# A convolution, Fourier and MLP kernel on one core: the front work of batches 2 to 7 put on batch 1's step table

## The chip, the cores and the metric

The kernel runs on one core of a Trainium2 chip. The metric is device time in microseconds (us). Before the change the median of three runs was 1313.27 us (1310.71 to 1316.33). One execution was profiled; its own time is 1317.36 us and its trace spans 1315.6 us.

## The reference, cut to what matters

For each of 8 batches of 4224 tokens with 192 channels, a causal convolution of 7 taps (softmax weights, one set per head of 24 channels) is followed by a two-dimensional Fourier transform whose real part is added back, a normalisation and a two-layer MLP with a residual:

```
x   = lightweight_conv(x, softmax(weight))          # (8, 4224, 192)
mix = real(fft(fft(x, axis=1), axis=2))
u   = x + mix
un  = (u - mean(u)) / sqrt(var(u) + 1e-6)            # over the 192 channels
out = u + relu(un @ w_ch1) @ w_ch2                   # 192 -> 768 -> 192
```

## The kernel before, in words

Work is cut into batches `b` (0 to 7) and, in each batch, nine items `it` (0 to 8). One item is 512 output tokens (item 8 has 128). A *step* `n = 9 b + it` is one pass of the loop at L882: the MLP of item `it` is its main work, and everything else is placed between the MLP's pieces. The MLP's first half (`mlp_hidden`, L665) makes six blocks `ph` of five matmuls each (L680); ScalarE writes each as `hh` (L684) and VectorE its remainder `hlo` (L685). Two PSUM buffers hold `ph`, so the sixth block cannot be computed before the fourth `hh` and `hlo` are written. The second half (`mlp_out`, L689) makes `po` (L699, L702, L705) one step later, from all six `hh` and `hlo`, adds it to `u` (L711) and stores `u` (L719). Normalisation (`un` L628, `hl` L638 and L641) and the DMA transpose of `hl` into `kt` (L651, on SyncE's queue, SP) run about two steps ahead of the MLP that reads `kt`.

The *front work* of a later batch rides in the steps of the batches ahead of it. `front(bt, rel)` (L763) says which pieces are issued in a step, by `rel = n - 9 b`:

- convolution of six window chunks (`load_windows` L323, matmuls `pc` L387, copies `xa` L395, stores to a DRAM scratch `sc` L355, squares `sq` L343) at rel -17 to -12; batch 7 does one head on VectorE instead (`conv_segments`, L403, stored by L421);
- `load_x` (L441): the scratch is read back in four pieces `xs` with another token order, four DMAs each on SP's queue (L456). The pieces share two buffers, so piece 2 can be loaded only when both splits of piece 0 are done, and piece 3 only after piece 1;
- `split_x` (L460): each piece is split in two halves into a high part `XH` (ScalarE, L472) and a low part `XL` (VectorE, L473), eight splits in all;
- `stage_a` (L479): 16 units of 12 matmuls `pa` (L490), written out as `yh` (ScalarE, L498) and `yl` (VectorE, L499). Each unit reads all of `XH` and `XL` in its columns, so none can start before the last split;
- `stage_b` (L504): matmuls `pb` (L516) into `V` (L524, L525), from rel -4 on by `b_at`.

Four tables set the steps of load, split and stage A. Batch 1 has its own (`load_1`, `split_1`, `a_1`); batches 2 to 7 use `load_at`, `split_at`, `a_at` (L752 to L754). Batch 0's are done before the loop. So batch 1's front work lies in the steps of batch 0, and that of batch 2 in the steps of batch 1. Below, "step 1 of batch 2" is item 1 of batch 2, where the front work of batch 3 has rel -8.

A scheduler turns this code into one instruction list per engine. It may move an instruction that is ready ahead of its place in the code, but each engine, and SP's queue of DMAs with it, then runs its list in order. `issue_after` keeps ScalarE's splits behind the last `hh` (L471) and, for batch 1 alone, loads behind the last transpose (L455).

## Time and profile before

| what | value |
|---|---|
| median of three runs | 1313.27 us |
| profiled execution, its own time | 1317.36 us |
| span of its trace | 1315.6 us |
| TensorE (PE) matmul busy | 1194.7 us, 91% |
| ScalarE (ACT) busy | 821.3 us, 62% |
| VectorE (DVE) busy | 746.8 us, 57% |
| GpSimd (POOL) busy | 645.0 us, 49% |
| mean granted TensorE clock | 0.961 |

The profiled execution is 1.8 us longer than its span and 4.1 us above the median. Matmuls are pipelined, so a busy PE is not a PE at its peak. Steps can be found in the trace by the first `hh` activation of each; from 429.7 us on, nine of them make batch 2. The granted clock is the share of full speed that TensorE had in a stretch.

### The profile page before, as it was taken

Reading aid. Unit: us, or ns where it says so; the run is one execution under the profiler, and the core shown is the slowest. Engines: PE = TensorE matmul, PEld = TensorE weight load, DVE = VectorE, ACT = ScalarE, POOL = GpSimd, SP = SyncE. Lnnn points to the kernel's source line nnn. Section 1 sums busy time; section 2 is a strip of 40 time slices with the busy share of each in tenths; the row PEclk is TensorE's granted clock in tenths of the full one; section 3 lists DMA queues with packets and bytes.
Section 4 is the critical chain, followed back from the end, with each engine's and each line's share of the span. In section 5 each row is a group of like instructions: output and inputs, shape, how many; then the busy total and the mean of one; then the engine's idle time right before and its main releaser. Section 6 shows DMA issues by size and latency. Waiting matters only on the chain.

```text
span 1315.6 us, 30115 instructions
## 1 busy us (share of the span) xinstructions
PE 1194.7 (91%) x12224; PEld 942.4 (72%) x12224; DVE 746.8 (57%) x1635; ACT 821.3 (62%) x1562; POOL 645.0 (49%) x1052
## 2 busy tenths in 40 slices
PE   4187899997999989997999979999889998999999
PEld 4175678775878668785777858787567876778667
DVE  6765564465545655456644565456754576555444
ACT  4655786566755687557765677566755667555642
POOL 0165644564445734455445563456434675456520
PEclk9587999998999989999999989999899999999999
DMA  8945865556756556466664557545564544223321
GB/s 271 247 118 136 226 161 120 133 117 142 146 127 132 150 117 133 121 139 149 124 147 109 134 152 146 133 117 145 136 123 117 124 101 85 72 68 76 76 64 40
DMA packets 225819, 170.19 MB, mean 129 GB/s; under 512 B 119560, under 2 KB 207440, under 8 KB 225680
## 3 DMA queue, kind: packets, MB, share of 16 engines
q1 hardware_dynamic: 163408, 108.53, 35.7%
q10 hardware_dynamic: 49600, 33.77, 10.5%
q0 software_dynamic: 12672, 25.97, 7.6%
q8 instruction: 95, 1.56, 0.5%
q14 instruction: 44, 0.36, 0.1%
HBM read 83.73 MB, written 58.55 MB: 108 GB/s over the span
## 4 chain that ended last, share of the span: by engine, by line
PE 38%; POOL 18%; issue 14%; ACT 11%; DMA 8%; DVE 5%; SPq 2%; ACTq 0%; POOLq 0%; DVEq 0%
PE ph L680 14%; POOL xr L544 8%; DMA xs<-sc 6%; PE po L699 4%; PE po L705 4%; PE po L702 4%; PE pa L490 4%; POOL u L592 4%; ACT XH L472 3%; PE pq L574 3%; POOL hl L641 3%; ACT un L628 2%; PE pc L387 2%; DVE XL L473 2%; PE pb L516 2%
## 5 line engine op out<-in xcount | busy, mean ns | idle before, releaser
L680 PE MATMUL ph<-kt,W 128*128 128x512 f16 (+1 forms) x2160 | 502.4, 366 | 19.5 <-DVE hlo L685 13.2
L685 DVE SCALAR_TENSOR_TENSOR hlo<-ph,hh 128x512 f16<-128x512 f32 (+1 forms) x400 | 271.5, 679 | 347.5 <-ACT hh L684 346.3
L699 PE MATMUL po<-W,hh 128*128 128x192 f16 x1584 | 388.7, 249 | 43.8 <-ACT hh L684 36.8
L702 PE MATMUL po<-W,hh 128*128 128x192 f16 x1584 | 388.5, 248 | 0.0
L705 PE MATMUL po<-W,hlo 128*128 128x192 f16 x1584 | 384.4, 248 | 0.8 <-DVE hlo L685 0.8
L684 ACT ACTIVATE hh<-ph 128x512 f16<-128x512 f32 (+1 forms) x400 | 235.3, 589 | 187.8 <-PE ph L680 180.0
L544 POOL DMA_INDIRECT xr<-sc,rows_sb x264 | 268.3, 1016 | 136.5 <-issue 59.4
L680 PEld LDWEIGHTS <-W 128*128 128x128 f16 x2160 | 195.3, 99 | 168.1 <-issue 29.4
L641 POOL TENSOR_TENSOR hl<-un,hl 128x512 f16<-128x512 f32 (+1 forms) x144 | 127.9, 910 | 219.2 <-ACT hl L638 219.1
L699 PEld LDWEIGHTS <-hh 128*128 128x128 f16 x1584 | 156.8, 99 | 58.6 <-ACT hh L684 40.0
L592 POOL TENSOR_TENSOR u<-u,xr 128x768 f32<-128x768 f32 (+1 forms) x72 | 124.6, 1731 | 138.2 <-ACT u L591 138.1
L705 PEld LDWEIGHTS <-hlo 128*128 128x128 f16 x1584 | 156.0, 99 | 26.0 <-issue 2.4
L702 PEld LDWEIGHTS <-hh 128*128 128x128 f16 x1584 | 156.4, 99 | 22.2 <-issue 7.8
L628 ACT ACTIVATE un<-u,nm,y 128x192 f32<-128x192 f32 x256 | 120.0, 537 | 73.1 <-POOL nm L618 72.7
L387 PE MATMUL pc<-xt,band 128*120 128x144 f32 x756 | 118.9, 297 | 21.8 <-DMA band<-line_d 14.7
L472 ACT ACTIVATE XH<-xs,s_x 128x768 f16<-128x768 f32 x64 | 104.3, 1670 | 40.3 <-DMA xs<-sc 40.3
L387 PEld LDWEIGHTS pc<-xt,band 128*120 128x120 f32 x756 | 105.6, 190 | 29.5 <-issue 14.7
L473 DVE SCALAR_TENSOR_TENSOR XL<-xs,s_x,XH 128x768 f16<-128x768 f32 x64 | 102.2, 1609 | 42.4 <-ACT XH L472 37.0
L490 PE MATMUL pa<-c_sb,XH 128*128 128x128 f16 x1024 | 103.1, 223 | 18.0 <-ACT XH L472 17.4
L711 DVE SCALAR_TENSOR_TENSOR u<-po,fo,u 128x384 f32<-128x384 f32 (+1 forms) x136 | 81.8, 601 | 58.1 <-PE po L705 57.0
L499 DVE SCALAR_TENSOR_TENSOR yl<-pa,yh 99x512 f16<-99x512 f32 x128 | 85.3, 681 | 33.2 <-ACT yh L498 33.2
L490 PEld LDWEIGHTS <-XH 128*128 128x128 f16 x1024 | 82.3, 99 | 28.1 <-ACT XH L472 18.0
(125 smaller groups left out, 1454.8 us busy)
## 6 DMA issues: line engine op xcount, KB each, us to landing
out_dram<-u SPq DMA_DIRECT2D x64, 384.0 KB
xt<-in_xw_dram SPq DMA_DIRECT2D x42, 576.0 KB
sc<-xa ACTq DMA_DIRECT2D x42, 540.0 KB
xs<-sc SPq DMA_DIRECT2D x96, 192.0 KB
xs<-sc SPq DMA_DIRECT2D x32, 216.0 KB
xr<-sc,rows_sb POOLq DMA_INDIRECT x264
sc<-xa ACTq DMA_DIRECT2D x7, 450.0 KB
xt<-in_xv_dram SPq DMA_DIRECT2D x6, 504.0 KB
```

The costliest lines, as they stand in the source:

```text
L387: nc.tensor.matmul(pc[:WR, h - h0], band[:, h, :WR], xt[:, :, h * GRP : (h + 1) * GRP], start=True, stop=True,)
L490: nc.tensor.matmul(pa[:, i], x[:, at], F[:, l], start=(n == 0), stop=(n == 2))
L544: nc.gpsimd.indirect_dma_start(bt.xr[it][:, g], None, bt.sc[:S], bass.IndirectOffsetOnAxis(ap=rows_sb[:, col : col + 1], axis=0),)
L592: nc.gpsimd.tensor_tensor(u[:, :ng], u[:, :ng], xr[:, :ng], op=ALU.add)
L628: nc.scalar.activation(un[:, g], u[:, g], AF.Identity, bias=nm[:, g : g + 1], scale=y[:, g : g + 1],)
L641: nc.gpsimd.tensor_tensor(bl[:, :, o : o + n], un[:, :ng, f], hi[:, :, f], op=ALU.subtract)
L680: nc.tensor.matmul(ph[:, n], W1[:, w, ht * 128 : (ht + 1) * 128], kt[:, k], start=(i == 0), stop=(i == len(order) - 1),)
L684: anchor[0] = nc.scalar.activation(hh, ph, AF.Relu).ins
L685: nc.vector.scalar_tensor_tensor(hlo, ph, 0.0, hh, op0=ALU.max, op1=ALU.subtract)
L699: nc.tensor.matmul(po[:, g % 2], hh[:, ht, tk], W2[:, ht, 0], start=(ht == 0), stop=False)
L702: nc.tensor.matmul(po[:, g % 2], hh[:, ht, tk], W2[:, ht, 1], start=False, stop=False)
L705: nc.tensor.matmul(po[:, g % 2], hlo[:, ht, tk], W2[:, ht, 0], start=False, stop=(ht == 5),)
```

## The change

Batches 2 to 7 get the tables that only batch 1 had, and batch 1's own copies of the three tables go. Load, split and stage A of those batches stand at rel -9 to -5 where they stood at -10 to -5: the first load and the first split one step later, stage A in two steps (6 and 10 units) where it had three (4, 6 and 6).

```diff
-    load_at = {-10: [0], -9: [1, 2], -8: [3]}
-    split_at = {-9: [0, 1], -8: [2, 3, 4, 5], -7: [6, 7]}
-    a_at = {-7: range(0, 4), -6: range(4, 10), -5: range(10, 16)}
+    load_at = {-9: [0, 1], -8: [2, 3]}
+    split_at = {-8: [0, 1], -7: [2, 3, 4, 5], -6: [6, 7]}
+    a_at = {-6: range(0, 6), -5: range(6, 16)}
...
-        conv, load, split, a = (
-            (conv_1, load_1, split_1, a_1) if bt.b == 1
-            else (conv_at, load_at, split_at, a_at)
-        )
+        conv = conv_1 if bt.b == 1 else conv_at
```

In the order of instructions, nothing changes on TensorE until the steps of batch 1. Three places show what moves. In the names, `hh_2_1` and `ph_2_1_3` are item 1 of batch 2 (and its block 3), and `xs_3_2` is piece 2 of batch 3's transform input.

ScalarE in step 1 of batch 2, before, from the second `hh` to the fourth:

```order
L684 ACTIVATE hh_2_1_5994<-ph_2_1_1_6071 128x512
L472 ACTIVATE XH_106<-xs_3_1_5925,s_x3_5555 128x64x12 x2
L610 ACTIVATE sd_2_4_6229<-mv_2_4_6140,eps_68 128x4
L684 ACTIVATE hh_2_1_5994<-ph_2_1_2_6129 128x512
L472 ACTIVATE XH_106<-xs_3_2_5941,s_x3_5555 128x64x12 x2
L628 ACTIVATE un_2_3_6004<-u_2_3_5894,nm_2_3_5981,y_2_3_5978 128x192 x4
L684 ACTIVATE hh_2_1_5994<-ph_2_1_3_6167 128x512
```

The same stretch after the change:

```order
L684 ACTIVATE hh_2_1_5985<-ph_2_1_1_6062 128x512
L472 ACTIVATE XH_106<-xs_3_0_5931,s_x3_5555 128x64x12
L610 ACTIVATE sd_2_4_6221<-mv_2_4_6132,eps_68 128x4
L684 ACTIVATE hh_2_1_5985<-ph_2_1_2_6123 128x512
L472 ACTIVATE XH_106<-xs_3_0_5931,s_x3_5555 128x64x15
L343 ACTIVATE sq_4_0_6161,nrm_4_6160<-xt_4_0_5772 128x1152
L395 ACTIVATE xa_4_0_6163<-pc_4_0_0_6164 120x3x6x24
L628 ACTIVATE un_2_3_5995<-u_2_3_5857,nm_2_3_5972,y_2_3_5969 128x192 x4
L684 ACTIVATE hh_2_1_5985<-ph_2_1_3_6169 128x512
```

Before, the splits of pieces 1 and 2 stand here, and the fourth `hh` stands behind those of piece 2. After, the two splits of piece 0 stand here, and piece 2 is not split before step 2.

SP's queue over steps 1 and 2 of batch 2, before (`kt` is a transpose, `xt` a window chunk of the convolution, `out` a store of `u`):

```order
L651 DMA_TRANSPOSE kt_2_2_5930<-hl_2_2_5847 128x12x128
L330 DMA xt_4_1_5992<-in_xw_dram 128x1152
L456 DMA xs_3_2_5941<-sc_3_3843 32x8x192 x4
L456 DMA xs_3_3_6066<-sc_3_3843 32x8x192 x4
L719 DMA out_1_dram<-u_2_0_5131 128x768
L651 DMA_TRANSPOSE kt_2_3_6124<-hl_2_3_6060 128x12x128
L330 DMA xt_4_2_6251<-in_xw_dram 128x1152
L651 DMA_TRANSPOSE kt_2_4_6365<-hl_2_4_6289 128x12x128
```

And after:

```order
L651 DMA_TRANSPOSE kt_2_2_5920<-hl_2_2_5810 128x12x128
L330 DMA xt_4_1_5983<-in_xw_dram 128x1152
L456 DMA xs_3_2_6057<-sc_3_3827 32x8x192 x4
L719 DMA out_1_dram<-u_2_0_5131 128x768
L651 DMA_TRANSPOSE kt_2_3_6118<-hl_2_3_6051 128x12x128
L330 DMA xt_4_2_6243<-in_xw_dram 128x1152
L651 DMA_TRANSPOSE kt_2_4_6342<-hl_2_4_6281 128x12x128
L456 DMA xs_3_3_6094<-sc_3_3827 32x8x192 x4
```

Piece 2's loads keep their place on SP, and piece 3's move back past a store, two transposes and a window load. Pieces 0 and 1 are read at the same places of SP's list in both programs.

ScalarE in step 2, where pieces 1 and 2 are split under the new table. In the program before, batch 1 has that table, so this is step 2 of batch 0:

```order
L684 ACTIVATE hh_0_2_1581<-ph_0_2_0_1583 128x512
L472 ACTIVATE XH_106<-xs_1_1_1310,s_x1_1273 128x64x12
L395 ACTIVATE xa_2_1_1719<-pc_2_1_0_1720 120x3x6x24
L395 ACTIVATE xa_2_1_1719<-pc_2_1_3_1737 120x3x6x24
L684 ACTIVATE hh_0_2_1581<-ph_0_2_1_1623 128x512
L472 ACTIVATE XH_106<-xs_1_1_1310,s_x1_1273 128x64x12
L472 ACTIVATE XH_106<-xs_1_2_1393,s_x1_1273 128x64x12
L610 ACTIVATE sd_0_5_1777<-mv_0_5_1692,eps_68 128x4
L684 ACTIVATE hh_0_2_1581<-ph_0_2_2_1681 128x512
```

Step 2 of batch 2 after the change:

```order
L684 ACTIVATE hh_2_2_6245<-ph_2_2_0_6247 128x512
L472 ACTIVATE XH_106<-xs_3_1_5959,s_x3_5555 128x64x12
L395 ACTIVATE xa_4_1_6383<-pc_4_1_0_6384 120x3x6x24
L395 ACTIVATE xa_4_1_6383<-pc_4_1_3_6401 120x3x6x24
L395 ACTIVATE xa_4_1_6383<-pc_4_1_6_6435 120x2x6x24
L355 DMA sc_4_6159<-xa_4_1_6383 120x6x192
L684 ACTIVATE hh_2_2_6245<-ph_2_2_1_6287 128x512
L472 ACTIVATE XH_106<-xs_3_1_5959,s_x3_5555 128x64x12
L472 ACTIVATE XH_106<-xs_3_2_6057,s_x3_5555 128x64x12
L355 DMA sc_4_6159<-xa_4_1_6383 120x3x192
L610 ACTIVATE sd_2_5_6441<-mv_2_5_6356,eps_68 128x4
L684 ACTIVATE hh_2_2_6245<-ph_2_2_2_6345 128x512
```

The splits stand at the same places between the `hh`; what differs is where the convolution's third `xa` and its two stores stand. On TensorE the two programs have the same work in these steps: 80 `po` (83 in batch 0) and no `pa` in step 2, 47 `po` and 82 `pa` in step 3, 83 `po` and 110 `pa` in step 4, 72 `po` and 31 `pb` in step 5. In the old order of batch 2 the `pa` of steps 2, 3 and 4 are 61, 79 and 52.

More of the change, by code (lines that the diff above doesn't have):

```diff
@@ L751 @@
     conv_at = {r: [r + 17] for r in range(-17, -11)}
-    load_at = {-10: [0], -9: [1, 2], -8: [3]}
-    split_at = {-9: [0, 1], -8: [2, 3, 4, 5], -7: [6, 7]}
-    a_at = {-7: range(0, 4), -6: range(4, 10), -5: range(10, 16)}
+    load_at = {-9: [0, 1], -8: [2, 3]}
+    split_at = {-8: [0, 1], -7: [2, 3, 4, 5], -6: [6, 7]}
+    a_at = {-6: range(0, 6), -5: range(6, 16)}
     b_at = {-4: [0], -3: [1, 2], -2: [3], -1: [4], 0: [5, 6], 1: [7]}
     conv_1 = {-9: [4, 5]}
-    load_1 = {-9: [0, 1], -8: [2, 3]}
-    split_1 = {-8: [0, 1], -7: [2, 3, 4, 5], -6: [6, 7]}
-    a_1 = {-6: range(0, 6), -5: range(6, 16)}
     def front(bt, rel):
         units = []
-        conv, load, split, a = (
-            (conv_1, load_1, split_1, a_1) if bt.b == 1
-            else (conv_at, load_at, split_at, a_at)
-        )
+        conv = conv_1 if bt.b == 1 else conv_at
         for ch in conv.get(rel, ()):
@@ L780, in front @@
             units.append(call(scales, bt))
-        units += [call(load_x, bt, ch) for ch in load.get(rel, ())]
-        units += [call(split_x, bt, i) for i in split.get(rel, ())]
-        units += [call(stage_a, bt, t) for t in a.get(rel, ())]
+        units += [call(load_x, bt, ch) for ch in load_at.get(rel, ())]
+        units += [call(split_x, bt, i) for i in split_at.get(rel, ())]
+        units += [call(stage_a, bt, t) for t in a_at.get(rel, ())]
         return units
```

## Prediction

> **What bounds the kernel now.** I read the page first, then cut batch 2 into its nine steps (at the first `hh` of each), then asked the waits and the chain of waits of the one step that stands out. The page gives TensorE (PE) as the busiest engine, and in the costliest groups one line on the part that the change moves, the splits:
>
> ```profile
> PE 1194.7 (91%) x12224; PEld 942.4 (72%) x12224; DVE 746.8 (57%) x1635; ACT 821.3 (62%) x1562; POOL 645.0 (49%) x1052
> L472 ACT ACTIVATE XH<-xs,s_x 128x768 f16<-128x768 f32 x64 | 104.3, 1670 | 40.3 <-DMA xs<-sc 40.3
> ```
>
> ScalarE (ACT) is only 62% busy, yet stood 40.3 us before splits because a load of `xs` had not landed. The steps of batch 2 (length, busy time by engine, granted clock) show where:
>
> ```profile
> 429.70:447.50 17.80, 17.63 (x201) 13.83 (x199) 11.06 (x24) 14.84 (x28) 11.50 (x20) 1.00 0.43 116
> 447.50:473.70 26.20, 17.71 (x130) 12.30 (x129) 13.76 (x23) 16.21 (x27) 14.29 (x23) 0.80 0.68 158
> 473.70:491.30 17.60, 17.60 (x183) 14.07 (x182) 11.32 (x23) 14.60 (x26) 7.14 (x12) 1.00 0.49 120
> 491.30:509.70 18.40, 18.40 (x196) 14.86 (x194) 11.29 (x25) 13.00 (x27) 8.96 (x14) 1.00 0.73 145
> 509.70:528.90 19.20, 19.20 (x206) 15.52 (x204) 10.41 (x23) 13.22 (x27) 8.97 (x14) 1.00 0.64 143
> 528.90:545.40 16.50, 16.50 (x177) 12.82 (x175) 6.59 (x13) 7.89 (x17) 6.87 (x15) 1.00 0.57 123
> ```
>
> The first number behind the length is PE's busy time. PE fills every step but step 1, which has few matmuls (130 records) and the longest time, with the clock at 0.80. The waits in that step, and the chain of waits through it:
>
> ```profile
> PE po L699 <- ACT hh L684: 7.4, 1, 7.4
> ACT XH L472 <- DMA xs<-sc: 7.0, 1, 7.0
> ```
>
> ```profile
> 446.82 1.92 DVE XL L473
> 448.76 0.33 SPq L456
> ...
> 452.20 8.44 DMA xs<-sc
> 460.80 3.09 ACT XH L472 x2
> ...
> 466.18 0.34 PE po L699
> ...
> 470.89 0.16 PE po L699
> ```
>
> This is a loop through two buffers. `XL` of piece 0 ends at 448.7, only then may SP issue piece 2 into its buffer, piece 2's split starts at 460.80, 12 us later, and the fourth `hh` stands behind that split on ACT; `po` waits for it until 466.18. Then PE runs at half speed: one `po` takes 0.16 us until past 470.89, against 0.08 in the same chain at full clock:
>
> ```profile
> 426.08 0.08 PE po L699
> 428.56 1.08 PE ph L680 x5
> 484.66 1.49 PE pc L387 x12
> ```
>
> So step 1 is not bound by PE's work but by one load that starts too late. The rows of step 1 for batches 1, 3, 4, 5 and 6:
>
> ```profile
> 291.00:317.00 26.00, 17.55 (x130) 12.29 (x129) 13.75 (x23) 16.20 (x27) 14.29 (x23) 0.80 0.69 159
> 604.20:628.30 24.10, 16.64 (x130) 11.69 (x129) 14.40 (x26) 16.23 (x27) 14.94 (x24) 0.86 0.68 164
> 758.90:782.30 23.40, 16.29 (x130) 11.62 (x129) 14.20 (x25) 16.29 (x27) 14.63 (x24) 0.85 0.65 165
> 912.70:934.70 22.00, 16.22 (x122) 10.88 (x120) 13.51 (x22) 14.22 (x24) 13.10 (x23) 0.84 0.74 180
> 1073.10:1093.30 20.20, 15.43 (x139) 11.23 (x137) 13.20 (x23) 14.89 (x24) 15.37 (x23) 1.00 0.66 129
> ```
>
> **The witness.** The old program already runs batch 1 on the new tables, inside the steps of batch 0. Its steps 1 to 5:
>
> ```profile
> 132.10:157.40 25.30, 21.06 (x199) 16.35 (x198) 13.14 (x36) 17.59 (x34) 14.24 (x27) 0.93 0.80 215
> 157.40:173.80 16.40, 14.75 (x117) 10.46 (x116) 12.59 (x21) 14.43 (x22) 10.58 (x13) 1.00 1.10 263
> 173.80:193.80 20.00, 19.91 (x221) 16.15 (x219) 13.16 (x25) 15.85 (x29) 7.76 (x13) 1.00 0.39 107
> 193.80:215.00 21.20, 21.20 (x239) 17.29 (x237) 12.84 (x27) 15.14 (x32) 10.75 (x16) 1.00 0.55 135
> 215.00:232.30 17.30, 17.30 (x190) 13.55 (x190) 7.12 (x13) 8.43 (x18) 6.85 (x15) 1.00 0.56 124
> ```
>
> Its step 1 is no model, since there the convolution and scale of batch 1 itself are still being finished. Steps 2 to 5 have the matmuls of the new order almost to the number. Its splits on ACT (start, length, in brackets the idle time before), and the issue of piece 3 on SP:
>
> ```profile
> 145.57 3.58 ACT L472 ACTIVATE XH<-xs,s_x 128x768 f16<-128x768 f32 x2 [3.29 <-DMA xs<-sc]
> 161.01 3.16 ACT L472 ACTIVATE XH<-xs,s_x 128x768 f16<-128x768 f32 x2
> 174.33 3.15 ACT L472 ACTIVATE XH<-xs,s_x 128x768 f16<-128x768 f32 x2
> ```
>
> ```profile
> 164.27 1.78 SPq L456 DMA_DIRECT2D xs<-sc  x4
> ```
>
> The 3.29 us is piece 0, whose scratch had only just been written. The first half of piece 2 (second in the row of 161.01) and piece 3 (174.33) started without a wait.
>
> **The change part by part,** for one batch.
>
> *Step 1: the wait goes.* Piece 0 is now split here and piece 2 one step later. Whether its load is then in time, ACT's own durations tell:
>
> ```profile
> 446.69 0.94 ACT L395 ACTIVATE xa<-pc 120x432 f32<-120x432 f32 x2
> ...
> 463.80 1.85 ACT L628 ACTIVATE un<-u,nm,y 128x192 f32<-128x192 f32 x4
> 465.55 0.57 ACT L684 ACTIVATE hh<-ph 128x512 f16<-128x512 f32 x1
> 466.03 1.15 ACT L343 ACTIVATE sq<-xt 128x1152 bf16<-128x1152 f32 x1
> ...
> 467.17 0.83 ACT L638 ACTIVATE hl<-un 128x768 f16<-128x768 f32 x1
> ...
> 470.39 1.21 ACT L591 ACTIVATE u<-pq,g 128x384 f32<-128x384 f32 x3 [1.91 <-DMA out_dram<-u]
> ```
>
> From the end of piece 0's second split to piece 2's first, ACT's new list has one `sq` (1.2), two sets of `un` (3.7), two `hl` (1.7), one `u` (1.2), five `hh` (2.5, a start every 0.5), six `xa` (2.8) and both splits of piece 1 (3.1): 16.2 us without any idle time. The load needs `XL` (1.9) and the 12.0 us from 448.76 to 460.80, together 13.9. So 7.0 us go. With the stand of 7.4 us the half clock behind it goes too: from 466.18 to between 471 and the step's end at 473.7, 4.9 to 7.5 us at half speed, which is 2.4 to 3.8 us lost; I take 3.0. The Trainium skill has this as a rule ("TensorE: Matmul & The Clock Gate", Part 1): about one idle window of 3.4 us drops the clock to half. Row and rule agree on a stand of 7.4 us; by the rule a remaining stand of over 3.4 us would bring the half clock back, and the second rival below prices that from rows.
> Step 1 takes in six `pc` (1.49/12 = 0.124 us each) and four `po` (0.08) from step 0, and a little ACT work in place of two splits: 1.1 to 1.5 us, I take 1.3. So 26.2 - 7.0 - 3.0 + 1.3 = 17.5 us. Bounds: 19.2 if only the wait goes (26.2 - 7.0), and 13.8 if PE's `ph`, `po` and `pc` alone set it (30 x 0.216 + 76 x 0.083 + 8 x 0.124).
>
> *Step 0: lighter.* It hands on 12 `po` and 6 `pc`: 12 x 0.083 + 6 x 0.124 = 1.7 us, and two splits of 1.6 us each on ACT, which PE hides there. I take -1.7 (bounds 0 and -1.9, the latter with the 0.2 us in which PE is idle there).
>
> *Steps 2 to 5: fuller.* Stage A's 16 units stand in two steps, right behind the last split, so PE has less to put between. The witness: 16.4 + 20.0 + 21.2 + 17.3 = 74.9 us against 17.6 + 18.4 + 19.2 + 16.5 = 71.7. That is +3.2, and includes PE waiting in step 3 for piece 3's splits. Steps 6 to 8 keep their work: 0.
>
> *Piece 3's load on SP.* It now stands behind two transposes and waits there for `XL` of piece 1. Queued behind it are a window load, a store and the transpose for the MLP three steps on, which the next step does not need. The witness left it 10.1 us (164.27 to 174.33), and it came in time. At the 12.0 us of piece 2's load it would be 1.9 us late. I take 0, the row of the same piece at the same place, and keep 1.9 per batch for the range. POOL takes no part in load, split or stage A, and no bytes or instructions are added.
>
> *Batch 7's head on VectorE.* Its tiles share the buffers of `xs`, so it moves along, and with it the issue that holds ACT in step 3 of batch 5:
>
> ```profile
> 956.72 4.75 ACTq L421 DMA_DIRECT2D sc<-sg  x1
> ```
>
> After the change this issue stands at the end of that step, with batch 7's first read of `xs` now ahead of a transpose on SP. I take 0, since the same issue stays in ACT's list; the bounds are 4.75 us either way, once in the run.
>
> *The sum.* Step 1 now: 26.0 + 26.2 + 24.1 + 23.4 + 22.0 + 20.2 = 141.9 us over six batches. After: 17.5 in batches 1 to 4, 17.0 in 5 (narrower convolution), 16.5 in 6 (none): 103.5. That gives -38.4. Step 0: five times -1.7 = -8.5 (batch 6 has no `pc` to move). Steps 2 to 5: six times +3.2 = +19.2. Together -27.7 us, from 1317.4 to 1289.7 for the profiled execution; on the median, which lies 4.1 us lower, 1313.3 - 27.7 = 1285.6.
>
> **Rivals.**
>
> *Full relief (0.12).* PE alone sets the new steps: step 1 at 15.5, and 2 to 5 at +1. Then -(141.9 - 93.0) - 8.5 + 6 = -51.4, so 1262. For it: PE is 91% busy and fills seven steps. Against: ACT's 16.2 us in step 1 shrink by little.
>
> *ACT keeps the bound (0.20).* The splits still stand ahead of `hh` in steps 1 and 2, PE still stands three to four microseconds, and the half clock comes back as in the witness's step 1 (0.93 of 25.3, 1.8 us). Step 1 at 19.2 in all six: -26.7 - 8.5 + 19.2 = -16.0, so 1297; with 0.9 us of wait for piece 3 it is 1303.
>
> *The late load moves to piece 3 (0.08, slower).* If piece 3's four DMAs need over 14 us, ACT stands before its splits in step 3, and stage A with it. All 7.0 + 3.0 us back in five batches is +50 - 28 = +22: 1335. It decides from about 3.9 us of wait a batch (with 1.7 of clock, 5 x 5.6 = 28). Against it: the witness's unharmed 10.1 us. The Trainium skill speaks for it ("DMA: Bandwidth & Descriptors", Rules for kernel authors): issue a DMA early, wait late. By that rule a table that loads later costs time. Here the issue of pieces 2 and 3 is set by the buffer's release, 448.7 in the chain, and what the table moves is mostly the reader; the trace so far speaks against the rule's use here.
>
> *Nothing to speak of (0.06).* The scheduler keeps its own order, pieces 0 and 1 are loaded at the same places as before, and gains and the fuller steps cancel: 1313.
>
> **How the numbers follow.** My forecast, 1285.6, has 0.54. About 0.5%, 6.6 us, is what a measurement here can tell from no change. Forecast, full relief and ACT's bound are all faster by more: 0.86. The same: 0.06. Slower: 0.08. The range runs from 1266 (most of full relief) to 1304 (ACT's bound with a late piece 3); outside lie the slower rival, no change and a part of full relief.
>
> **What would show it.** In the changed profile, step 1 of batches 1 to 5 should last 16 to 19 us with the clock near 1.00, and ACT's wait for `xs` before splits should fall from 40.3 to under 15 us (the first batches keep theirs). Steps 3 and 4 should be 19 to 22 us. If step 1 shrinks and step 3 shows ACT waiting for `xs`, the third rival is right; if step 1 stays above 19 with no DMA wait, the second. I am wrong if steps 2 to 5 grow by over 8 us.

## The result and the profile after

The changed kernel takes 1300.77 us, the median of four runs (1298.91 to 1301.58), beside 1313.15 us for the kernel before on the same chip: a ratio of 0.990 with an interval of 0.988 to 0.992. Forecast were 1285.6 us, in a range of 1266 to 1304. So the direction is right and the time lies in the range, but the gain is 12.4 us where the sum gave 27.7. The profiled execution took 1301.58 us with a span of 1299.8 us, 15.8 us less than the span before. The page of the changed kernel, the busy engines and the row of the splits:

```profile
PE 1192.8 (92%) x12224; PEld 937.5 (72%) x12224; DVE 745.3 (57%) x1635; ACT 821.3 (63%) x1562; POOL 649.5 (50%) x1052
L472 ACT ACTIVATE XH<-xs,s_x 128x768 f16<-128x768 f32 x64 | 105.7, 1681 | 16.8 <-DMA xs<-sc 16.8
```

ScalarE's wait for loads ahead of splits fell from 40.3 to 16.8 us. TensorE is busy as long as before (1192.8 against 1194.7 us), so what was gained is idle time of TensorE. The steps 0 to 5 of batch 2 after the change (length, busy time by engine, granted clock), to be laid beside the six rows before:

```profile
421.50:436.10 14.60, 14.60 (x174) 11.05 (x173) 8.58 (x22) 10.82 (x24) 9.37 (x17) 1.00 0.46 130
436.10:456.80 20.70, 19.06 (x170) 15.16 (x168) 9.81 (x19) 15.29 (x28) 13.02 (x24) 1.00 0.57 128
456.80:472.90 16.10, 13.17 (x101) 8.46 (x100) 12.64 (x21) 14.26 (x23) 9.22 (x13) 1.00 1.13 194
472.90:494.60 21.70, 19.96 (x218) 15.97 (x216) 13.11 (x25) 15.73 (x28) 7.68 (x13) 1.00 0.56 139
494.60:515.90 21.30, 21.30 (x241) 17.39 (x239) 12.84 (x27) 15.19 (x32) 10.73 (x16) 1.00 0.52 137
515.90:533.10 17.20, 17.20 (x188) 13.44 (x188) 7.13 (x13) 8.37 (x17) 6.83 (x15) 1.00 0.59 119
```

Length less the first busy number is TensorE's idle time. In step 1 it was 8.49 us and is 1.64, and the clock there is 1.00: the stand is gone. But step 1 is not 17.5 us long, because TensorE has 19.06 us of work in it (170 matmul records, 130 before), taken by the scheduler from steps 0 and 2. And there is new idle time: 2.93 us in step 2 and 1.74 in step 3, where there was none. In batch 4 the half clock is back as well, in steps 2 and 3:

```profile
762.30:778.70 16.40, 14.25 (x102) 9.58 (x101) 12.64 (x21) 14.40 (x23) 9.51 (x13) 0.90 1.13 174
778.70:803.40 24.70, 21.78 (x203) 17.27 (x201) 13.29 (x25) 15.94 (x29) 7.42 (x13) 0.86 0.51 118
```

Since the scheduler moves TensorE's work from step to step, the length of a step misleads. I therefore cut batches 1 to 6 of each profiled kernel into their 54 steps and summed, by step, length less busy time of TensorE. All numbers are us over six batches; the last column is the length of the six batches, steps 5 to 8 have 2.2 us of idle time together in new_rstd_on_dve and 0.5 or less in the others, and the ratio is to the kernel before timed on the same chip beside it.

| kernel | ratio | step 0 | step 1 | step 2 | step 3 | step 4 | all idle | TensorE busy | length |
|---|---|---|---|---|---|---|---|---|---|
| before | 1 | 0.9 | 42.1 | 3.4 | 4.6 | 0.0 | 51.4 | 871.4 | 922.7 |
| the change | 0.990 | 0.1 | 10.3 | 16.5 | 10.1 | 2.0 | 38.9 | 872.5 | 911.4 |
| after_again | 0.991 | 0.1 | 11.4 | 18.1 | 9.8 | 1.9 | 41.3 | 871.6 | 912.9 |
| old_three_buffers | 0.997 | 1.7 | 34.7 | 4.3 | 2.3 | 2.9 | 46.2 | 873.3 | 919.5 |
| old_piece2_late | 0.996 | 0.5 | 30.9 | 14.8 | 6.9 | 2.8 | 56.2 | 871.9 | 928.1 |
| old_gathers_late | 0.997 | 3.4 | 31.8 | 0.6 | 5.7 | 0.0 | 41.5 | 872.3 | 913.8 |
| old_three_gathers_late | 0.992 | 4.7 | 33.0 | 3.9 | 0.0 | 0.0 | 41.6 | 870.2 | 911.8 |
| old_one_gather | 0.953 | 0.0 | 21.0 | 2.7 | 0.1 | 0.0 | 23.8 | 861.5 | 885.3 |
| new_three_buffers | 0.985 | 2.0 | 11.6 | 19.7 | 3.9 | 0.6 | 37.9 | 869.6 | 907.5 |
| new_three_again | 0.987 | 1.5 | 11.6 | 19.8 | 3.5 | 0.4 | 36.9 | 873.3 | 910.2 |
| new_three_split_323 | 0.995 | 1.9 | 18.0 | 11.7 | 5.4 | 6.8 | 43.7 | 877.5 | 921.2 |
| new_three_hl_dve | 0.989 | 0.5 | 12.9 | 21.3 | 3.9 | 0.5 | 39.1 | 873.1 | 912.2 |
| new_three_gathers_early | 1.007 | 4.0 | 24.1 | 23.8 | 2.6 | 0.0 | 54.8 | 874.8 | 929.6 |
| new_rstd_on_dve | 1.002 | 4.7 | 21.5 | 19.0 | 5.7 | 4.3 | 57.3 | 881.0 | 938.3 |
| new_one_gather | 0.965 | 0.0 | 19.8 | 11.6 | 2.2 | 3.4 | 37.1 | 869.7 | 906.8 |
| new_one_gather_u6 | 0.952 | 0.0 | 0.0 | 12.5 | 8.1 | 3.1 | 23.7 | 860.6 | 884.3 |
| new_u6 | 0.990 | 0.1 | 11.6 | 17.9 | 11.2 | 2.5 | 43.2 | 870.2 | 913.5 |

Each row is one execution; that of new_one_gather is the slowest of its four (1293.1 us, median 1285.1). The kernel before took 1313.2 us beside the changed kernel, 1315.2 us beside after_again and the three kernels with gathers late or early, and 1330 to 1332 us beside all others; so times are compared by their ratios alone. The kernel before has a profile on the first of these chips only. What a slower chip adds seems to lie ahead of batch 1: new_u6, which has the ratio of the changed kernel, begins batch 1 at 279.1 us in place of 269.3, and its span is longer by the same 9.9 us (1309.7 against 1299.8). The six batches can therefore be compared, with that one pair as the evidence.

### The profile page after: what moved, and what is told of

Same layout as the page of the kernel before. It is cut to its first block, busy times and chain, and to the rows that moved or that the text cites. A ratio compares the mean times of both kernels' runs of the same rounds, so it can differ in the third digit from the quotient of the medians.

```text
span 1299.8 us, 30094 instructions
## 1 busy us (share of the span) xinstructions
PE 1192.8 (92%) x12224; PEld 937.5 (72%) x12224; DVE 745.3 (57%) x1635; ACT 821.3 (63%) x1562; POOL 649.5 (50%) x1052
## 4 chain that ended last, share of the span: by engine, by line
POOL 27%; PE 24%; issue 19%; ACT 12%; DMA 8%; DVE 6%; SPq 1%; ACTq 1%; POOLq 0%; DVEq 0%
POOL xr L544 12%; PE ph L680 9%; DMA xs<-sc 5%; POOL u L592 5%; POOL hl L641 4%; PE pa L490 4%; ACT un L628 4%; ACT XH L472 3%; DVE XL L473 2%; PE po L699 2%; PE po L702 2%; PE po L705 2%; DMA sc<-xa 2%; PE pq L574 2%; PE pc L387 2%
## 5 line engine op out<-in xcount | busy, mean ns | idle before, releaser
L680 PE MATMUL ph<-kt,W 128*128 128x512 f16 (+1 forms) x2160 | 500.8, 366 | 16.3 <-DVE hlo L685 10.3
L544 POOL DMA_INDIRECT xr<-sc,rows_sb x264 | 267.3, 1013 | 131.4 <-issue 60.4
L592 POOL TENSOR_TENSOR u<-u,xr 128x768 f32<-128x768 f32 (+1 forms) x72 | 121.1, 1683 | 158.1 <-ACT u L591 154.6
L387 PE MATMUL pc<-xt,band 128*120 128x144 f32 x756 | 114.2, 293 | 21.8 <-DMA band<-line_d 14.9
L490 PE MATMUL pa<-c_sb,XH 128*128 128x128 f16 x1024 | 101.9, 224 | 25.8 <-ACT XH L472 22.2
L387 PEld LDWEIGHTS pc<-xt,band 128*120 128x120 f32 x756 | 101.5, 186 | 28.3 <-issue 14.8
L473 DVE SCALAR_TENSOR_TENSOR XL<-xs,s_x,XH 128x768 f16<-128x768 f32 x64 | 102.4, 1607 | 30.9 <-ACT XH L472 24.8
L472 ACT ACTIVATE XH<-xs,s_x 128x768 f16<-128x768 f32 x64 | 105.7, 1681 | 16.8 <-DMA xs<-sc 16.8
```

The costliest lines, as they stand in the source:

```text
L387: nc.tensor.matmul(pc[:WR, h - h0], band[:, h, :WR], xt[:, :, h * GRP : (h + 1) * GRP], start=True, stop=True,)
L490: nc.tensor.matmul(pa[:, i], x[:, at], F[:, l], start=(n == 0), stop=(n == 2))
L544: nc.gpsimd.indirect_dma_start(bt.xr[it][:, g], None, bt.sc[:S], bass.IndirectOffsetOnAxis(ap=rows_sb[:, col : col + 1], axis=0),)
L592: nc.gpsimd.tensor_tensor(u[:, :ng], u[:, :ng], xr[:, :ng], op=ALU.add)
L680: nc.tensor.matmul(ph[:, n], W1[:, w, ht * 128 : (ht + 1) * 128], kt[:, k], start=(i == 0), stop=(i == len(order) - 1),)
```

## The experiments

The kernels whose names begin with old_ are the kernel before with an edit, those with new_ the changed kernel with one.

### The loop through two buffers

The first theory was the prediction's: step 1 stood because two loader buffers let piece 2's load start too late. A third buffer takes that wait away without moving anything in the tables (the same edit at all five places of the tag):

```diff
-        tag, bufs = (("yh", 1), ("yl", 1))[i - 2] if b == 0 and i > 1 else ("xs", 2)
+        tag, bufs = (("yh", 1), ("yl", 1))[i - 2] if b == 0 and i > 1 else ("xs", 3)
```

> The old tables with three buffers for xs in place of two; the lists of PE and ScalarE stay as they were, and on SP only piece 2's loads move ahead. Theory (the stand in step 1 is the loop through two buffers): ScalarE's wait for piece 2 goes, step 1 falls from 20-26 us to 16-19 us with the clock at 1.00, steps 2 to 5 stay at 71.7 us, and the time falls to 1265-1280 us, below the changed kernel. Rival (step 1 is over-full on ScalarE and GpSimd whatever the load does): step 1 falls only to 21 us or above, as in the changed kernel, and the time stays at 1285 us or above.

Measured: 1327.17 us beside 1330.72, ratio 0.997 (0.995 to 0.999), step 1 at 22.1 us in batch 2. ScalarE does not wait for a load in step 1 any more, yet the theory fell. In the waits of that step stands another one:

```profile
ACT un L628 <- POOL nm L618: 4.3, 1, 4.3
```

and GpSimd's list in that step, gathers of residual rows (`xr`, L544) and the normalisation of item 3 (L611 to L618):

```profile
460.93 0.19 POOL L614 TENSOR_TENSOR t<-y 128x4 f32<-128x4 f32 x1
461.28 1.06 POOL L544 DMA_INDIRECT xr<-sc,rows_sb  x1 [0.16 <-POOL t L614]
462.64 0.95 POOL L544 DMA_INDIRECT xr<-sc,rows_sb  x1 [0.30 <-issue]
463.89 1.86 POOL L544 DMA_INDIRECT xr<-sc,rows_sb  x1 [0.30 <-issue]
466.06 1.17 POOL L544 DMA_INDIRECT xr<-sc,rows_sb  x1 [0.30 <-issue]
467.25 1.34 POOL L615 TENSOR_TENSOR t<-t,w 128x4 f32<-128x4 f32 x1
...
470.87 0.20 POOL L618 TENSOR_TENSOR nm<-nm,y 128x4 f32<-128x4 f32 x1
```

Four gathers of 0.95 to 1.86 us stand inside a chain of operations that mostly take 0.2 us, and `un` can start only at 471.11. The same chain stands in the kernel before, hidden: there its last part ends just ahead of the load.

```profile
456.06 1.17 POOL L544 DMA_INDIRECT xr<-sc,rows_sb  x1 [0.30 <-issue]
...
458.60 0.20 POOL L618 TENSOR_TENSOR nm<-nm,y 128x4 f32<-128x4 f32 x1
```

`nm` is ready at 458.8, the load at 460.8, and `un`, the next in ScalarE's list that needs `nm`, starts at 463.80 behind two splits. Had the load come at once, `un` could have started at 458.8 at the earliest: 2.0 of the 7.0 us would have stayed as a wait for GpSimd, and with the third buffer, where GpSimd's operations come later still, 4.3 did. In the list of waits only the later of two is seen.

Batch 6 of the kernel before shows the second wait by itself. No convolution runs in its step 1, and ScalarE waits for no load there, but it does wait for `nm`:

```profile
ACT un L628 <- POOL nm L618: 3.6, 1, 3.6
```

That step is 20.2 us long, with the clock at 1.00.

Putting two of the splits one step later in the old tables was another way to take the reader away from the load:

```diff
-    split_at = {-9: [0, 1], -8: [2, 3, 4, 5], -7: [6, 7]}
+    split_at = {-9: [0, 1], -8: [2, 3], -7: [4, 5, 6, 7]}
```

> The old tables, and only the two splits of piece 2 stand one step later (rel -7 where they stood at -8); stage A keeps its three steps. Theory (what the change is worth is that piece 2's reader moves away from its load; what it costs is stage A in two steps): step 1 falls to 17-20 us, step 2 grows by 1 to 3 us, 3 to 5 stay, 1270-1285 us. Rival (four splits and stage A in step 2 cost what step 1 gives): step 2 above 23 us, 1295 us or above.

Measured: 1326.73 us, ratio 0.996 (0.995 to 0.998): step 1 at 21.4 us in batch 2, steps 2 and 4 at 19.6 and 20.5. The gain is a fraction of what the theory asked for. TensorE's idle time in step 1 fell from 42.1 to 30.9 us and rose in step 2 from 3.4 to 14.8.

In the changed kernel the third buffer tests something else, the late load of piece 3:

> The changed kernel with three buffers for xs. Theory (step 3 is longer than the witness's because piece 3 is loaded late): ScalarE's waits of 1.8 to 3.0 us in step 3 go, step 3 is 20 us or less in batches 1 to 4, the half clock in batch 4 goes too, 8 to 15 us in all: 1286-1293 us. Rival (stage A in two steps sets step 3): step 3 stays at 21 us or above and the time within 5 us of 1300.8.

Measured: 1312.14 us, ratio 0.985 (0.981 to 0.988). The steps 3 of batches 1 to 4, 21.1 to 24.7 us in the changed kernel, are 20.0 to 20.3, and TensorE's idle time in the six steps 3 from 10.1 to 3.9 us. This part of the theory stands. A second measurement of the same kernel:

> The changed kernel with three loader buffers, unaltered (0.985 of the time before in the first call), beside the other kernels of this call. Theory (the third buffer takes away the waits for piece 3's load in step 3 of batches 1 to 5, at which TensorE idled for 1.7 us in batch 2 and lost its full clock in batch 4): ratio 0.983 to 0.988, so 0.3 to 0.7 per cent below the changed kernel. Rival (0.985 came from that chip's slower kernel before): 0.990 or more.

Measured: 1314.74 us, ratio 0.987 (0.983 to 0.991). Step 3 of batch 2 has 0.06 us of idle time (19.90 us long, 19.84 busy).

With the two measurements this is the best kernel of the study that leaves nothing out, 0.3 to 0.6 per cent below the changed kernel; the intervals of the two touch or overlap, and they were not timed side by side. Most of what step 3 gave came back elsewhere: with the third buffer the idle time of steps 0 rose by 1.9 us and that of steps 2 by 3.2, so that the six batches have 37.9 and 36.9 us of it in the two measurements and 38.9 in the changed kernel.

### GpSimd's list

If the chain on GpSimd is late by itself, it should help to take its small operations off GpSimd.

```diff
-        G_ = nc.gpsimd
+        G_ = nc.vector
```

> The changed kernel with the seven small operations of the normalisation (L611 to L618) on VectorE in place of GpSimd, so that they no longer stand between gathers. Theory (step 1 at 20.6 us is set by ScalarE's list, which waits about 1.2 us for GpSimd twice): step 1 falls by 1 to 2.5 us, elsewhere the waits of about 1 us for nm go too, 1285-1296 us. Rival (step 1 is PE's own work): step 1 unchanged, and the time within 3 us of 1300.8, or longer by VectorE's extra work.

Measured: 1334.12 us, ratio 1.002 (1.000 to 1.003), so 1.2 per cent more than the change. TensorE's idle time is 57.3 us. The wait for the chain did shrink, from 76.0 us in the whole run to 30.8, and in step 1 of batches 1 to 4 it is gone. But another wait of ScalarE stands there instead, for a store that must empty a buffer of `u`; in the whole run of the changed kernel it is 0.4 us, and here

```profile
ACT u L591 <- DMA out_dram<-u: 36.8, 7, 8.6
ACT un L628 <- DVE nm L618: 30.8, 36, 2.4
```

In the steps 1 of batches 1 to 4 it is 6.6, 7.6, 8.6 and 7.8 us. In batch 2 that store is issued at 465.22, right behind the four issues of piece 2's load (463.24). The kernels with fewer gathers, below, meet the same wait and take it away; this kernel was not run with a sixth buffer for `u`.

The other way is to move the gathers. With

```diff
-            place(gathers(n + 4), 1, 2)
+            place(gathers(n + 4), 7, 1)
```

in the kernel before, and `0, 1` in the changed one with three loader buffers, no gather stands inside item 3's chain in batches 1 to 5.

> The kernel before with one edit: the four gathers of a step's residual rows are placed behind the seventh unit of the step and on, not behind the first, third, fifth and seventh, so that on GpSimd the normalisation chain of item 3 stands whole and no gather stands inside it. Two loader buffers as before. Theory (in step 1 two waits end almost together: ScalarE's wait for the load of piece 2, and behind it the normalisation chain on GpSimd among the gathers; taking one away leaves the other): step 1 stays at 24 to 26 us in batches 1 to 4 and the ratio to before lies between 0.994 and 1.004. Rival 1 (the chain on GpSimd alone sets step 1): step 1 at 22 us or less, ratio 0.985 or less. Rival 2 (later gathers come too late for the residual add): steps grow by 1 us or more all over, ratio above 1.01.

Measured: 1311.36 us beside 1315.23, ratio 0.997 (0.996 to 0.999), as the theory said, but not for its reason. Step 1 fell to 20.1 to 20.9 us without any other edit, the number of the first rival, and ScalarE's waits in it hold no load:

```profile
447.10:467.20 20.10, 15.35 (x125) 10.97 (x122) 14.26 (x22) 16.61 (x27) 15.11 (x19) 0.92 0.73 147
```

Batches 1 to 4 take 152.4 to 152.8 us each, where batches 1 to 3 take 152.2 to 153.2 after the change. What is lost again lies elsewhere: step 0 is 1.1 us longer in each batch, and batch 1 starts at 275.6 us, not 273.2. The load's wait thus went with an edit that touches no load. In the window of that load the kernel before has the convolution's stores (`sc<-xa`, two of 540 KB) on a queue that is empty in the other; the queues q1 and q10 of the kernel before, 440 to 462 us:

```profile
q1 hardware_dynamic: 3631, 2.37, 45.9%
q10 hardware_dynamic: 1470, 1.11, 20.8%
```

and of old_gathers_late in the same stretch:

```profile
q1 hardware_dynamic: 2641, 2.19, 42.8%
```

The gathers (a queue of their own, q0) move the same 0.79 MB in both. In the kernel before, the stores are issued at 448.4, just ahead of piece 2's load, and three of its four issues on SP take 1.07, 1.92 and 2.08 us; in old_gathers_late the stores are issued at 464.3, and the four issues take 0.3 to 0.5 us. Two more stretches fit: step 1 of batch 6 of the kernel before has no stores, and step 1 of batch 2 of old_one_gather issues them at 446.3, behind its load; in both no issue of a piece takes over 0.46 us. That piece 2's load was slow because of the stores beside it is still an argument from these rows; no run moves the stores alone.

> The kernel before with both edits: three loader buffers (alone 0.997, step 1 at 22.1 us, of which 4.3 us are ScalarE's wait for GpSimd's normalisation chain) and the gathers behind the seventh unit. Theory of the two waits: both are gone now, step 1 falls by about the 4.3 us to 17.5 to 18.5 us in batches 1 to 5, the ratio is 0.978 to 0.985. Rival (ScalarE's and TensorE's own lists fill step 1, with the wait only a place where the engine stands): step 1 stays at 20.5 us or more, ratio 0.992 or more.

Measured: 1305.57 us, ratio 0.992 (0.991 to 0.994), step 1 at 21.2 to 22.2 us in batches 1 to 5. The theory's 17.5 to 18.5 us did not come, the rival's 20.5 or more did: TensorE still idles for 33.0 us in the six steps 1. But it is not ScalarE or TensorE that fills them. In the chain of waits through step 1 of batch 2 the gathers have 28.6% and the split `hl` on GpSimd 13.8%, the two largest shares: a gather that does not stand inside the chain stands ahead of it.

> The changed kernel with three loader buffers (alone 0.985, step 1 at 18.8 us) and the gathers placed behind the first, second, third and fourth unit of the step, by which on GpSimd no gather stands inside the normalisation chain of item 3. Theory of the two waits: ScalarE's wait for the chain (1.2 us in the changed kernel) goes, step 1 at 17.3 to 18.3 us, ratio 0.978 to 0.984. Rival (the chain is covered by other work there already): step 1 at 18.6 us or more, ratio 0.985 or more.

Measured: 1325.79 us, ratio 1.007 (1.004 to 1.009). Neither came: the time is longer than before the change. Step 1 of batch 2 is 20.5 us, step 0 18.9, and idle time is 54.8 us. ScalarE's wait for the chain in step 1 grew from 1.2 to 3.0 us, behind four gathers that now stand ahead of the chain, and the wait for the store of `u` stands there too: 4.3 to 7.5 us in the steps 1 of batches 1 to 5.

> The changed kernel itself, unaltered, on the chip of the other kernels of this call, as their reference. Both theories: ratio 0.988 to 0.992, with steps 0 to 5 of batch 2 within 0.5 us of 14.6, 20.7, 16.1, 21.7, 21.3 and 17.2. If the waits for piece 3's load in step 3 came from chance in one execution, step 3 of batches 1 to 4 would be at 20.5 us or less in this one.

Measured: 1300.67 us, ratio 0.991 (0.988 to 0.994). Steps 1 and 3 of batch 2 are 20.6 and 22.2 us, and the steps 3 of batches 1 to 4 are 21.5 to 23.3: the waits for piece 3 are no chance.

A smaller relief of GpSimd:

```diff
-            nc.gpsimd.tensor_tensor(
+            (nc.gpsimd if n == 128 else nc.vector).tensor_tensor(
```

> The changed kernel with three loader buffers and with the second, smaller subtraction of the split of the normalised rows (64 columns of each group) on VectorE in place of GpSimd: about 1.2 us less on GpSimd for each of the 64 items, in steps where VectorE has 9.8 of 18.8 us busy. Theory (GpSimd's list holds steps 1 and 2): those steps shorten by 0.5 to 1.5 us a batch against the same kernel without this edit, ratio 0.3 to 0.7 per cent lower than that one's in this call. Rival (what leaves GpSimd's list lands in VectorE's, ahead of the statistics and of the lows of the hidden layer): no gain or a loss, ratio as high or up to 1 per cent higher.

Measured: 1316.35 us, ratio 0.989 (0.986 to 0.992), no gain over the 0.987 of new_three_again, timed beside it: the rival.

### What the gathers cost

Two kernels issue one gather for each step in place of four and add its rows to all four groups (three quarters of the residual sum are left out):

```diff
-        nc.gpsimd.tensor_tensor(u[:, :ng], u[:, :ng], xr[:, :ng], op=ALU.add)
+        nc.gpsimd.tensor_tensor(
+            u[:, :ng], u[:, :ng], xr[:, 0:1].to_broadcast([128, ng, D]), op=ALU.add
+        )
...
-        return [call(load_res, bt, it, g) for g in range(1 if it == Q0 else 4)]
+        return [call(load_res, bt, it, g) for g in range(1)]
```

> The kernel before with one gather for each step in place of four (three quarters of the residual sum are left out), loads and tables as before. Theory (two waits end almost together in step 1, and the gathers lengthen both: the chain by standing in it, the load by their transfers, since with the gathers placed later the load's wait went with the chain): step 1 at 21 us or less in batches 1 to 4 without any change of the tables, ratio 0.975 to 0.987. Rival (the load of piece 2 is late by itself, because its buffer comes free late): step 1 at 23 us or more, with ScalarE's wait for it of 4 us or more, ratio 0.992 or more.

Measured: 1267.89 us beside 1331.63, ratio 0.953 (0.950 to 0.956), a larger gain than the theory's end of 0.975. The old tables stay, and step 1 is 18.8 to 19.0 us:

```profile
430.70:449.70 19.00, 15.85 (x118) 11.03 (x116) 13.59 (x23) 15.73 (x25) 9.30 (x16) 0.91 0.59 135
```

ScalarE still waits for piece 2's load there, but 1.7 us in place of 7.0; the stores have moved behind that load, so this fall is not the gathers' own work alone. The six batches are 37 us shorter. The rest of the gain lies outside them (the loop's first `hh` is at 106.5 us, and at 117.3 in the kernel before on another chip).

> The changed kernel with one gather of residual rows for each step in place of four: the first group's rows are added to all four groups, so three quarters of the residual sum are left out and the time says only what the gathers cost. TensorE's idle time in steps 1 and 2 of a batch is 4.5 us in the changed kernel (1.64 and 2.93 us in batch 2). Theory (it is GpSimd's list, with the four gathers of about 1 us each ahead of and inside the normalisation chain, that holds ScalarE and through it TensorE there): the idle time of the two steps falls to 2.5 us or less, steps 1 and 2 together from 36.7 to 35 us or less, and the whole to a ratio of 0.975 to 0.983. Rival (the two steps are held by ScalarE's own work, 15.3 and 14.3 us of it, and by the buffer of un): the two steps stay at 36.2 us or more, ratio 0.987 or more.

Measured: 1285.10 us, timed beside old_one_gather, ratio 0.965 (0.962 to 0.968). The ratio is lower than the theory's, but the two steps are not: 20.5 and 16.5 us, the rival's number. And it is slower than the old tables with the same gathers. The reason is a third wait in step 1, the one of new_rstd_on_dve:

```profile
ACT u L591 <- DMA out_dram<-u: 5.6, 1, 5.6
```

The store of an older `u` stands on SyncE's queue behind piece 2's four issues, which wait for `XL` of piece 0 until 444.65; it is issued at 446.52 and lands 6.9 us later. The chain of waits in that step:

```profile
442.74 1.91 DVE XL L473
...
446.02 0.45 SPq L456
446.47 0.05 issue
446.52 0.02 SPq L721
446.54 0.04 issue
446.58 6.90 DMA out_dram<-u
...
453.59 1.22 ACT u L591 x3
```

(Line numbers from L592 on are higher by two in this kernel, so L721 is the store of L719.) A sixth buffer for `u` takes this wait away:

> The changed kernel with one gather for each step in place of four (three quarters of the residual sum are left out; alone 0.965, steps 1 and 2 of batch 2 at 20.5 and 16.5 us) and six buffers in place of five for the residual sum u. Theory (with the gathers gone a third wait stands in step 1: ScalarE waits 5.6 us, in batch 5 10.1 us, for the store that must empty a buffer of u, and that store stands on SyncE behind the four issues of piece 3's load, which the change moved into this step): with a sixth buffer the wait goes, step 1 at 18.5 us or less in batches 1 to 5, the ratio 0.945 to 0.958. Rival (step 1 is filled by TensorE's and ScalarE's own work at 20 us): step 1 at 20 us or more, ratio 0.962 or more.

Measured: 1267.41 us beside 1330.09, ratio 0.952 (0.950 to 0.954). Step 1 of batch 3 has no idle time at all, and step 2 keeps its own:

```profile
580.80:596.70 15.90, 15.90 (x140) 12.31 (x140) 9.98 (x19) 13.96 (x25) 7.51 (x14) 1.00 0.51 113
596.70:612.80 16.10, 13.92 (x115) 9.98 (x113) 12.34 (x21) 13.89 (x20) 8.49 (x11) 1.00 1.10 245
```

The theory is confirmed: in step 1 the load, GpSimd's chain and the store of `u` lay one behind the other, and of all the kernels here only the one with all three out of the way has no idle time of TensorE there. One word of it was wrong: what stands ahead of the store is piece 2's load, by the rows above, and not piece 3's.

> The changed kernel with its four gathers and six buffers for u. Theory (in the changed kernel itself the normalisation chain on GpSimd is the later of the two and covers the wait for the store; its trace shows no wait of ScalarE for a store in step 1): the same as the changed kernel, ratio 0.987 to 0.994, step 1 at 20 to 21 us. Rival (the store, not GpSimd's chain, holds step 1 there): step 1 at 19 us or less, ratio 0.982 or less.

Measured: 1313.54 us beside 1330.09, ratio 0.990 (0.986 to 0.993), as the theory said. Step 1 is 18.7 to 18.8 us in batches 2 to 5, the rival's number, but its idle time is unchanged (11.6 us for 10.3); the work went to step 8, which is 9.5 to 10.0 us long in place of 7.9. Here lengths alone would have misled.

### Step 2

What holds step 2 of the changed kernel was tried with three loader buffers and the splits laid otherwise:

```diff
-    split_at = {-8: [0, 1], -7: [2, 3, 4, 5], -6: [6, 7]}
+    split_at = {-8: [0, 1, 2], -7: [3, 4], -6: [5, 6, 7]}
```

> The changed kernel with three loader buffers (0.985 and 0.987, TensorE idle 19.7 us in the six steps 2 of batches 1 to 6) and the eight splits of a batch laid 3, 2 and 3 over steps 1, 2 and 3 in place of 2, 4 and 2. Theory (step 2 of the changed kernel is held by ScalarE's own list: 14.3 of its 16.1 us busy, two splits in a row ahead of the third set of hidden values): with two splits fewer there TensorE's idle time in the six steps 2 falls from 19.7 to 10 us or less, and the ratio to 0.978 to 0.984. Rival (the idle time only moves to steps 1 and 3, where the splits go): idle of steps 1 to 3 together stays at 32 us or more (35.3 without this edit), ratio 0.985 or more.

Measured: 1324.22 us beside 1331.5, ratio 0.995 (0.993 to 0.997). Idle time in the six steps 2 fell from 19.7 to 11.7 us, in steps 1 it rose from 11.6 to 18.0, and steps 1 to 3 have 35.0 us together, 35.3 without the edit: the rival. Where the splits go, the idle time goes too, and 6.8 us of it are in steps 4, 0.6 without the edit. That ScalarE's splits are what holds TensorE in step 2 fits this and is not shown by it, since a wait for the store of `u` (15.5 us in the whole run, 3.3 without the edit) came with the edit.

## Why the prediction was wrong

**What was right.** The stand of step 1 was ScalarE's, the change takes the wait for piece 2's load away in batches 1 to 5, and the clock of step 1 comes back to 1.00. The 17.5 us held 26.2 - 17.71 - 7.0 = 1.5 us of idle TensorE for each batch, 9 over six; measured are 10.3. That ScalarE's own list ahead of piece 2's split would be long enough for the load was right too. The signs that the prediction had named point several ways at once: step 1 stays above 19 us with no wait for a load, which was to mean the second rival; ScalarE waits for `xs` in step 3, which was to mean the third; its wait for `xs` before splits fell to 16.8 us and not under 15.

**Where the sum failed, in lengths.** For steps 0, 1, 2 to 5 and 6 to 8 the forecast was -8.5, -38.4, +19.2 and 0, together -27.7. Measured over the same six batches: -18.3, -18.8, +26.4 and -0.6, together -11.3; ahead of batch 1 another 3.9 us went, and 0.6 in batch 7. The first two terms are both far off, half of it against each other: the scheduler laid 13.0 us more of TensorE's work into the six steps 1 than before (112.8 against 99.8 us busy), and took 17.5 out of steps 0 and 20.9 out of steps 2. I had moved 1.3 us a batch into step 1. So the 17.5 us were wrong as a length, by 3 us a batch, for work that was only moved. In batch 6 the sum took off 3.7 us (20.2 to 16.5) for a wait that was not there: in that step 1 ScalarE waited for GpSimd's `nm` and for no load. After the change it measured 19.9 us.

**Where it failed, in idle time.** The step that failed is "Steps 2 to 5: fuller", with its witness, and with it the 0 for piece 3's load. The witness has 16.40 - 14.75 = 1.65 us of idle TensorE in step 2 and 0.09 in step 3, 10.4 us over six batches. Measured are 28.6 in steps 2 to 4. With step 1's 9 the forecast left 19.4 of 51.4 us, so its -27.7 was 32.0 us less idle time and 4.3 us more work; the profile has 38.9 left, 12.5 us less idle time and 1.1 us more work. The 19.5 us of idle time that did not go are more than the whole miss of 27.7 - 11.3 = 16.4 us in these batches. They have two places:

- *Step 3, 10.1 us where the witness has 0.5.* 8.0 us of it lie in batches 1 to 4, where piece 3's load is late by 1.1, 1.8, 2.3 and 3.0 us; the rest is in batches 5 and 6, at waits for VectorE's `yl` and `XL`. I had named 1.9 us as the bound and taken 0. On SyncE's queue the four issues stand behind a transpose, in the witness and in batch 2 after the change:

```profile
161.65 1.71 SPq L651 DMA_TRANSPOSE kt<-hl  x1
```

```profile
461.01 4.35 SPq L651 DMA_TRANSPOSE kt<-hl  x1
465.45 2.75 SPq L456 DMA_DIRECT2D xs<-sc  x4
```

and ScalarE starts the split late:

```profile
475.26 3.13 ACT L472 ACTIVATE XH<-xs,s_x 128x768 f16<-128x768 f32 x2 [1.77 <-DMA xs<-sc]
```

  In the witness the queue was free at 163.4 and the buffer at 164.2, so the transpose cost nothing. In batch 2 `XL` of piece 1 had set the buffer free at 464.1, 1.3 us ahead of the first issue. Counted from the first `hh` of step 2, the load starts at 6.9 us in the witness and at 8.65 here, and has about the same time from there to its split (10.1 and 9.8 us): it is late because it starts late. In new_three_buffers the four issues start at 461.97, ahead of step 2 and of both transposes, and step 3 has 1.0 us of idle time in batches 1 to 4 (3.9 in all six): so this is shown for step 3, though not how much of it is the buffer's and how much the transpose's. This is the rival "the late load moves to piece 3" in small; I gave it 0.08 as an alternative, where it was a part of the likely case. In batch 4 it also brought the half clock back (0.86 in step 3). The Trainium skill's rule that I had set aside there, to issue a DMA early and wait for it late ("DMA: Bandwidth & Descriptors", Rules for kernel authors), names the direction that the trace took: the load whose issue moved back is the one that is late, by 1.1 to 3.0 us.

- *Step 2, 16.5 us where the witness has 9.9.* Four splits stand in it, and ScalarE is busy for 14.26 of 16.1 us. The two splits in a row, the third `hh` behind them and TensorE's wait for it:

```profile
460.93 3.17 ACT L472 ACTIVATE XH<-xs,s_x 128x768 f16<-128x768 f32 x2
463.99 0.28 ACT L610 ACTIVATE sd<-mv,eps 128x4 f32<-128x4 f32 x1
464.18 0.58 ACT L684 ACTIVATE hh<-ph 128x512 f16<-128x512 f32 x1
```

```profile
464.82 0.26 PE L699 MATMUL po<-W,hh 128*128 128x192 f16 x1 [0.95 <-ACT hh L684]
466.38 1.24 PE L680 MATMUL ph<-kt,W 128*128 128x512 f16 x5 [1.22 <-DVE hlo L685]
```

  With fewer gathers it still is 12.5 us, with splits moved away the idle time moves along. So it reads as the cost of having four splits in a step of little TensorE work, which is argued from these rows and not shown by a run. It would then be the rival "ACT keeps the bound", which named steps 1 and 2 and laid its price in step 1; that its 1297 to 1303 us hold the measured time is chance, since it had step 1 at 19.2 us and the step measures 20.5. I had seen the 1.65 us in the witness and not asked whose they were.

**The half clock.** I took 3.0 us a batch as regained. Batches 2 and 5 are without any half clock after the change. TensorE's busy time fell from 147.91 to 146.10 us in batch 2, by 1.8, and from 148.44 to 145.09 in batch 5, where the clock had been 0.93 in step 3 as well. In batches 1, 3, 4 and 6 the clock fell elsewhere (0.81 to 0.90 in step 2), and over six batches the busy time is the same to 1.1 us. So this term came to nothing on the whole.

In step 2 of batch 4 two short stands sufficed for it. TensorE's waits there:

```profile
770.34 0.26 PE L699 MATMUL po<-W,hh 128*128 128x192 f16 x1 [0.92 <-ACT hh L684]
771.91 1.69 PE L680 MATMUL ph<-kt,W 128*128 128x512 f16 x5 [1.23 <-DVE hlo L685]
```

and the granted clock in stretches of 2 us behind them (1.00 again from 776 on):

```profile
772.00:774.00 2.00, 2.00 (x9) 0.92 (x9) 2.00 (x3) 1.41 (x3) 1.82 (x3) 0.64 0.61 54
774.00:776.00 2.00, 2.00 (x13) 1.69 (x12) 0.51 (x1) 1.98 (x5) 0.00 (x0) 0.51 1.31 151
```

In batch 2 the same two waits, 0.95 and 1.22 us, left the clock at 1.00. The Trainium skill's one idle window of about 3.4 us ("TensorE: Matmul & The Clock Gate", Part 1), from which I expected the half clock behind a stand of over 3.4 us, does not say when the clock falls in this trace.

**What the prediction did not see at all.** It said that GpSimd takes no part in load, split or stage A. That is so, and yet GpSimd set how much a load was worth: part of the 7.0 us of wait in step 1 was covered a second time by its chain, 2.0 us by the rows before and 4.3 with a third buffer, and in the changed kernel the chain of waits through step 1 runs over its gathers:

```profile
439.79 0.20 POOL t L615
439.99 0.15 issue
440.14 1.07 POOL xr L544
...
446.80 0.17 POOL y L617
446.97 0.15 POOL t L614
447.12 0.16 POOL nm L618
447.28 0.03 issue
447.31 0.03 ACT un L628
```

With one gather a step the old tables reach 0.953 and the new ones 0.965; the change is then a loss of 1.3 per cent, and with the sixth buffer for `u` (0.952, a buffer that the old tables were not run with) it is worth nothing. So the gain of the later load hangs on the gathers that stand beside it, and not on the load alone. The second wait could have been read ahead of the change in step 1 of batch 6, whose length and clock the prediction shows and whose waits it does not.

**What stays open.** Why the four issues of piece 2's load took from 448.8 to 454.3 us in the kernel before and 0.3 to 0.5 us each in old_gathers_late is argued above and not shown. What holds step 2 is argued too. Whether the small operations on VectorE would pay once the store of `u` is out of the way (new_rstd_on_dve with six buffers) was not tried. Whether the gathers cost by their time on GpSimd (192 fewer of them took 179 us off its 645) or by their transfers was not separated.

## What to carry to other kernels

A wait in the trace names only the last of the things that were waited for. Before a wait is put into a sum as gained, look on every engine and queue that feeds the same reader for the moment when its part was ready; the gain ends at the next of these. An edit that takes one wait away and gains nothing (new_rstd_on_dve) may only have uncovered the next. And where a scheduler moves work between steps, sum the idle time of the bound engine rather than the lengths of steps; a witness for a moved step has to be read for its idle time too, and a load whose issue moves back is late until its row shows otherwise.

## What the runs showed of the hardware

- A gather of 128 rows by index holds GpSimd for 1.0 us (264 of them, 1013 ns in the mean). An operation of the normalisation on 128x4 elements takes 0.2 us there; right behind a gather one took 1.34 us (old_three_buffers).
- After the change a DMA transpose took 1.42 us to issue on SyncE's queue in step 0 of batch 2, 5.75 us in step 1 and 4.35 us in step 2, and the issues behind it on that queue began after it.
- In step 2 of batch 4 the granted clock fell to 0.64 and 0.51 behind two stands of TensorE of 0.92 and 1.23 us; in batch 2 stands of 0.95 and 1.22 us left it at 1.00.
- The same kernel before took 1313 to 1315 us beside some of these kernels and 1330 to 1332 us beside others, a difference as large as the change's gain.
